# A new order table for the attention stages ahead of and inside a fused attention and MLP kernel

## The chip, the cores and the metric

The kernel runs on one core of a Trainium2 chip. The metric is the device time of one execution in microseconds (us), as a median of several runs.

## The reference

```python
def _attn_ref(q, k, v, p):                       # batch 8, heads 8, seq 576, head_dim 64, 32 packs
    p_packed = sm_attn(p, k, v)                  # 32 packed queries attend to all keys
    return sm_attn(q, p_packed, p_packed)        # all queries attend to the 32 packed rows

def _moe_ref(x, w_gate, w_val, w_out, rms_g):    # 4608 tokens, 512 -> 1536 -> 512
    xn = x / sqrt(mean(x * x) + 1e-6) * rms_g
    g = xn @ w_gate
    return (g * sigmoid(g) * (xn @ w_val)) @ w_out

def _moe2_ref(x, w_in, w_out):                   # 512 -> 2048 -> 512
    h = x @ w_in
    return maximum(0.01 * h, h) @ w_out
```

`reference()` runs the three one after the other. `sm_attn` is the scaled softmax attention; q, k and p are drawn eight times wider than v. The weights come in double precision.

## The kernel before

**Three stretches.** First come the loads, the attention of the first batches and the conversion of the first weights (here called the front). Then a main loop of 96 steps (L1207) forms the first MLP: four pairs of batches, six groups of 256 hidden columns each, two batches and two halves of a sequence. Last comes the second MLP as a matrix product with fewer multiplications, from tiles that the main loop prepared. Every product is made of three: a value is split into a rounded high part and a low part (`mm3`, `split`).

**Units.** The attention of a batch is cut into two units of four heads, so there are 16 units. `soft1` (L324) is a unit's first attention, nine stages: keys, packs, scores, exps, sums, turn, packed, packed_turn, factors. `soft2` (L468) is the second: queries, scores, maxima, shift, exps, sums, norm, turn, two squares, and for a batch's second unit means and two finals. Stages issue loads too: keys loads the next unit's k and p, queries the next q, packed the next v. From batch 1's end on, shift, norm and final run on GpSimd.

**What goes beside it.** `split_w` and `split_wo` take one tile of weights each: `convert` (L683) turns doubles into floats, one ScalarE instruction (L693) and four on VectorE (L696, L702, L713, L719); the load of a later tile follows. `fold` (L872) multiplies weights by the packed rows (pwps) and splits the result (pw), ScalarE first, VectorE last. It uses the same PSUM banks as the output products y (`y_out`, L936). `split_at` splits the attention weights that the products g and v (`gv`, L913) read. `keep_warm(n)` (L960) issues n dummy products, two matmul instructions each.

**The order.** Each stage has a step number. `ONE` and `TWO` hold those of `soft1` and `soft2`, unit by unit; SPLITW, SPLITO, FOLD0, FOLD, SPLITA and WARM those of the rest. Units 8 to 15 follow a formula:

```python
S1 = (0, -2, 2, 6, 10, 11, 13, 15, 17)
S2 = (4, 5, 6, 7, 8, 8, 10, 12, 16, 17, 22, 25, 23)
L0, LP = 78, 23
ONE += tuple(tuple(L0 + LP * i + at for at in S1) for i in range(8))
TWO += tuple(tuple(L0 + LP * (i + 1) + at for at in S2[: 10 + 3 * (i % 2)]) for i in range(8))
```

`fill_slots` (L644) enters the stages in a table, and `run_slots(end)` (L652) traces all below `end` in order of step; within a step the units come first, then dummies, split_at, weights, folds. Steps below zero are traced in one go before the main loop. In the loop `slot()` (L1013) is called four times in each of the 96 main-loop steps, so main-loop step n covers steps 4n to 4n + 3. Folds of the later pairs, the conversion of the second MLP's weights and later split_at are called from the loop itself, outside the tables.

The order of tracing is a priority. A planner at compile time orders each engine's queue with estimated times and lets ready work of later steps go first. Two calls bind it: `tc.keep_in_program_order` pins an instruction behind the one that its engine was handed last (the dummies, and before the loop the first instruction of each conversion), and `tc.issue_after` puts what follows behind a given instruction. At run time each engine works through its queue in order and waits on semaphores. All loads and stores that matter here are issued from SP's queue.

Of the kernel before, what the change touches and what calls it, by code (L numbers as in the profile page):

```python
# [15 lines left out]
DRAM = bass.MemoryType.DRAM  # L16


S1 = (0, -2, 2, 6, 10, 11, 13, 15, 17)
S2 = (4, 5, 6, 7, 8, 8, 10, 12, 16, 17, 22, 25, 23)  # L20

ONE = (
# [8 lines left out]
)  # L31
TWO = (
# [8 lines left out]
)  # L41
L0, LP = 78, 23
ONE += tuple(tuple(L0 + LP * i + at for at in S1) for i in range(8))
TWO += tuple(tuple(L0 + LP * (i + 1) + at for at in S2[: 10 + 3 * (i % 2)]) for i in range(8))
SPLITW = (-68, -58, -57, -57, -8, -6, -1, -1, 9, 10, 13, 13, 21, 29, 29, 29, 37, 37, 45, 42, 50, 53, 59, 61,)
SPLITO = (-56, -63, 3, 8, 26, 29, 33, 39, 48, 55, 67, 71,)
FOLD0 = (-36, -31, 4, 0,)
FOLD = (4, 5, 23, 31, 36, 44, 60, 55, 63, 79,)
SPLITA = (-5, -18,)
WBUFS = 8  # L50
HEAD = 2
OWN = 1
# [8 lines left out]
CUT = 3  # L61
CONV0, CONV = 25, 1.6
EVERY = (1, 1)
WARM = ([-90, 5], [-58, 5], [-49, 10], [-22, 1],)


@with_exitstack
def pack_attention_moe_kernel(
# [592 lines left out]
    def split_at(b, cs=(0, 1)):  # L661
        if b not in ath:
            ath[b] = (
                mlpa.tile([P, 2, S], F32R, tag="ath", bufs=2, name=f"ath{b}"),
                mlpa.tile([P, 2, S], F32R, tag="atl", bufs=2, name=f"atl{b}"),
            )
        h, l = ath[b]
        f = atf[b]
        assert {("at", b, 0), ("at", b, 1)} <= made
        for c in cs:  # L670
            cs = slice(c * CH, c * CH + CH)
            act_copy(h[:, :, cs], f[:, :, cs])
            sub(side[0], l[:, :, cs], f[:, :, cs], h[:, :, cs])
# [107 lines left out]
    def split_w(i):  # L781
        if i < NW:
            until(lambda: ("r", i) in wq)
            t = mlpa.tile([P, 512], F32, tag="w", bufs=WBUFS, name=f"w{i}")
            convert(wq.pop(("r", i)), t, f"w{i}", True)

            def done():
                wq["s", i] = t
                flush_store()
                stores.append((w_dram[i], t))  # L790
                if i >= 2:
                    load_w(i + 2)

            after(done)
        elif i < NPAIR * NW:
            t = mlpa.tile([P, 512], F32, tag="w", bufs=WBUFS, name=f"w{i}")
            nc.sync.dma_start(out=t, in_=w_dram[i % NW])
            wq["s", i] = t
# [14 lines left out]
    def split_wo(i):  # L813
        if i < NF1:
            until(lambda: ("r", i) in wo)
            t = mlpb.tile([P, 2, 512], F32R, tag="wo", bufs=4, name=f"wo{i}")
            convert(wo.pop(("r", i)), t, f"wo{i}")

            def done():
                wo["s", i] = t  # L820
                flush_store()
                stores.append((wo_dram[i], t))
                if i >= 1:
                    load_wo(i + 1)

            after(done)
        elif i < NPAIR * NF1:
            t = mlpb.tile([P, 2, 512], F32R, tag="wo", bufs=4, name=f"wo{i}")
            ins = nc.sync.dma_start(out=t.bitcast(F32), in_=wo_dram[i % NF1])
            tc.keep_in_program_order(ins)  # L830
            wo["s", i] = t
# [40 lines left out]
    def fold(n, u, bbs=(0, 1)):  # L872
        if n >= NPAIR * NFG:
            return
        ks = [n * KT + 2 * u + x for x in range(2)]
        until(lambda: all(("s", k_) in wq for k_ in ks))
        w = [wq["s", k_] for k_ in ks]
        outs = []
        for bb in bbs:
            if (n, bb) not in pw:  # L880
                pw[n, bb] = mlpa.tile(
                    [P, 2, 2, 2 * G * P], F32R, tag=f"pw{bb}", bufs=2, name=f"pw{n}{bb}"
                )
            outs.append(bank(f"pwps{n}{u}{bb}")[:, 0, :])
            assert ("lpw", 2 * (n // NFG) + bb, u) in made
        def part(h, bb, ps):
            r = (h ^ bb) % 2
            rs = slice(64 * r, 64 * r + 64)
            c = 32 * (h % 2)
            return nc.tensor.matmul(  # L890
                ps[32 * h : 32 * h + 32],
                lhsT=lpw[2 * (n // NFG) + bb][rs, 2 * u + h // 2, c : c + 32],
                rhs=w[h // 2][rs],
                start=True,
                stop=True,
            )

        todo = [(h, bb, ps) for h in range(4) for bb, ps in reversed(list(zip(bbs, outs)))]
        with claim(outs[:-1]):
            first = part(*todo[0])  # L900
        with tc.issue_after(first.ins):
            for x in todo[1:]:
                part(*x)
        for bb, ps in zip(bbs, outs):
            hi, lo = pw[n, bb][:, u, 0, :], pw[n, bb][:, u, 1, :]
            act_copy(hi, ps)
            sub(nc.vector, lo, ps, hi)
# [52 lines left out]
    def keep_warm(count):  # L960

        ps = psA.tile([P, 512], F32, tag="y", bufs=4, name="warm")
        for _ in range(count):
            ins = nc.tensor.matmul(
                ps[:, :256],
                lhsT=ident,
                rhs=mask.rearrange("p h d -> p (h d)"),
                start=True,
                stop=True,
            )  # L970
            tc.keep_in_program_order(ins)

    for k_, count in WARM:
        slots.setdefault(k_, []).append(lambda count=count: keep_warm(count))
# [8 lines left out]
    halves = [(lambda c=c: split_at(0, (c,))) for c in range(2)]  # L983
    table = list(zip(SPLITA, halves))
    table += [(k_, lambda i=i: split_w(i)) for i, k_ in enumerate(SPLITW)]
    table += [(k_, lambda i=i: split_wo(i)) for i, k_ in enumerate(SPLITO)]
    table += [(k_, lambda i=i: fold(0, i % 2, (i // 2,))) for i, k_ in enumerate(FOLD0)]
    table += [(k_, lambda i=i: fold(1 + i // 2, i % 2)) for i, k_ in enumerate(FOLD)]
    for k_, f_ in table:
# [486 lines left out]
```

## Time and profile before

| | us |
|---|---|
| median of 3 runs (1636.6, 1639.88, 1641.48) | 1639.88 |
| the profiled execution | 1636.23 |
| its span, first to last instruction | 1634.5 |
| TensorE (PE) busy | 1547.3 |
| VectorE (DVE) busy | 1117.9 |
| ScalarE (ACT) busy | 764.7 |
| GpSimd (POOL) busy | 598.5 |

The profile is of one execution. Times below are from the start of the span. In a timeline each row has start, duration, engine, line, operation, tiles (out<-in), shapes, count, and in brackets the idle time of the engine just before and what ended it. PE are the matmuls and PEld their weight loads; SPq is the queue that issues loads. TensorE's clock as granted is given as a share of 2.4 GHz, so 0.50 is 1.2 GHz.

### The profile page before, as it was taken

To read this page: it belongs to the slowest core of one execution; us is meant where nothing else is said; L and a number is where in the kernel's file an instruction comes from. 1 tells how busy PE (TensorE), PEld (TensorE's weight loads), DVE (VectorE), ACT (ScalarE), POOL (GpSimd) and SP (SyncE) were. 2 spreads that over 40 slices of the span, in tenths; PEclk is the share of its full clock that TensorE was granted. 3 is DMA by queue.
4 is the path that set the end of the run, shared out by engine and by line. 5 is a ranking of instruction groups with operands and counts; after the bars stand their busy time and mean duration, and the time that the engine had idled before them with its cause. 6 is when DMAs were issued, how large, how long until landed. Compare 5 with 4: busy or idle time off the path is not lost.

```text
span 1634.5 us, 29463 instructions
## 1 busy us (share of the span) xinstructions
PE 1547.3 (95%) x10760; PEld 1363.4 (83%) x10760; DVE 1117.9 (68%) x2026; ACT 764.7 (47%) x1390; POOL 598.5 (37%) x415
## 2 busy tenths in 40 slices
PE   6789889999999899999999999999999999999997
PEld 4458778878888788888999988888889998999997
DVE  7787888566767756677768549646854964784475
ACT  3365544464445554555434246346524633553452
POOL 1124334443434524355224463075017306502610
PEclk8799999999999999999999999999999999999999
DMA  8664554375556834468775666787787778778776
GB/s 264 208 185 154 187 168 132 116 231 177 174 171 220 267 108 149 162 219 312 257 262 210 225 203 201 210 287 201 204 266 241 218 228 276 212 213 255 215 212 176
DMA packets 219519, 342.22 MB, mean 209 GB/s; under 512 B 21232, under 2 KB 120560, under 8 KB 219376
## 3 DMA queue, kind: packets, MB, share of 16 engines
q1 hardware_dynamic: 217488, 339.42, 66.0%
q8 instruction: 86, 1.41, 0.4%
q10 hardware_dynamic: 1888, 0.92, 0.2%
q14 instruction: 57, 0.47, 0.1%
HBM read 266.86 MB, written 73.40 MB: 208 GB/s over the span
## 4 chain that ended last, share of the span: by engine, by line
PE 66%; DVE 14%; DMA 9%; ACT 4%; issue 3%; POOL 2%; SPq 1%; ACTq 0%; DVEq 0%; POOLq 0%
PE o L142 22%; PE h L142 20%; PE y L142 11%; PE g L142 5%; PE v L142 4%; DMA sl<-c_dram 2%; DVE y_acc L952 2%; DMA wo<-in_moe_w_out_dram 2%; DMA w<-in_moe_w_in_dram 1%; PE pwps L890 1%; DMA w<-in_moe_w_out_dram 1%; PE xp L566 1%; DMA pc<-s_dram 1%; DVE pw L167 1%; DVE cvw L713 1%
## 5 line engine op out<-in xcount | busy, mean ns | idle before, releaser
L142 PE MATMUL o<-gh,pc 128*128 128x448 f32 (+1 forms) x1120 | 324.6, 371 | 0.0
L142 PE MATMUL y<-hh,wo 128*128 128x288 f32 x1536 | 274.0, 301 | 20.4 <-DVE pw L167 13.6
L142 PE MATMUL h<-yh,pc 128*128 128x448 f32 (+1 forms) x1120 | 280.7, 372 | 4.5 <-DMA pc<-s_dram 2.6
L142 PEld LDWEIGHTS y<-hh,wo 128*128 128x128 f32 x1536 | 223.7, 189 | 50.3 <-DVE pw L167 15.1
L167 POOL TENSOR_TENSOR hl<-sg,hh 128x576 fp32r<-128x576 f32 x96 | 146.9, 1530 | 293.1 <-ACT hh L159 284.9
L142 PEld LDWEIGHTS h<-yh,pc 128*128 128x128 f32 x1120 | 209.7, 188 | 31.3 <-ACT b5h L159 2.9
L142 PEld LDWEIGHTS o<-gh,pc 128*128 128x128 f32 x1120 | 210.2, 188 | 25.0
L159 ACT ACTIVATE gh<-g 128x448 fp32r<-128x448 f32 (+1 forms) x280 | 160.8, 587 | 131.4 <-PE o L142 68.9
L167 DVE TENSOR_TENSOR gl<-g,gh 128x448 fp32r<-128x448 f32 (+1 forms) x280 | 180.2, 661 | 50.0 <-ACT gh L159 42.9
L142 PE MATMUL o<-gl,pc 128*128 128x448 f32 (+1 forms) x560 | 207.0, 371 | 0.0
L1300 POOL TENSOR_TENSOR b6h<-b6h,b5h 128x448 f32<-128x448 f32 (+1 forms) x40 | 59.0, 1475 | 348.7 <-ACT gh L159 262.9
L952 DVE TENSOR_TENSOR y_acc<-y_acc,y 128x288 f32<-128x288 f32 x320 | 139.1, 446 | 55.0 <-PE y L142 54.1
L142 PE MATMUL y<-hl,wo 128*128 128x288 f32 x768 | 164.4, 296 | 1.2 <-POOL hl L167 1.2
L142 PE MATMUL h<-yl,pc 128*128 128x448 f32 (+1 forms) x560 | 162.7, 371 | 0.0
L142 PE MATMUL g<-ath,pw 128*128 128x288 f32 x768 | 152.3, 307 | 8.4 <-ACT sg L1240 6.1
L142 PE MATMUL v<-ath,pw 128*128 128x288 f32 x768 | 145.4, 302 | 1.4 <-DVE sg L929 1.4
L142 PEld LDWEIGHTS g<-ath,pw 128*128 128x128 f32 x768 | 115.9, 189 | 31.0 <-issue 12.2
L142 PEld LDWEIGHTS y<-hl,wo 128*128 128x128 f32 x768 | 123.8, 189 | 2.3 <-POOL hl L167 2.3
L1294 POOL TENSOR_TENSOR g<-g,g 128x448 f32<-128x448 f32 (+1 forms) x80 | 116.1, 1451 | 25.0 <-ACT gh L159 13.2
L142 PEld LDWEIGHTS v<-ath,pw 128*128 128x128 f32 x768 | 115.8, 189 | 4.7 <-DVE sg L929 2.5
L142 PEld LDWEIGHTS h<-yl,pc 128*128 128x128 f32 x560 | 105.1, 188 | 12.3
L142 PEld LDWEIGHTS o<-gl,pc 128*128 128x128 f32 x560 | 105.1, 188 | 12.3
(162 smaller groups left out, 2452.6 us busy)
## 6 DMA issues: line engine op xcount, KB each, us to landing
pc<-s_dram SPq DMA_DIRECT2D x320, 256.0 KB, 3.0
pc<-w_dram SPq DMA_DIRECT2D x240, 256.0 KB, 3.0
w<-w_dram SPq DMA_DIRECT2D x72, 256.0 KB, 4.1
wo<-wo_dram SPq DMA_DIRECT2D x36, 512.0 KB, 5.1
w_dram<-w2s SPq DMA_DIRECT2D x32, 512.0 KB, 4.9
s_dram<-ss SPq DMA_DIRECT2D x32, 512.0 KB, 6.0
v<-in_v_dram SPq DMA_DIRECT2D x16, 576.0 KB, 4.9
y_dram<-y_acc SPq DMA_DIRECT2D x32, 288.0 KB, 2.6
```

Source lines behind the costliest of these rows:

```text
L142: mm = nc.tensor.matmul(ps, lhsT=lh if a == "h" else ll, rhs=rh if b == "h" else rl, start=start and i == 0, stop=stop and i == n - 1,)
L159: nc.scalar.activation(out=o, in_=i, func=AF.Copy, scale=scale)
L167: eng.tensor_tensor(out=o, in0=a, in1=hi.bitcast(F32), op=ALU.subtract)
L566: nc.tensor.matmul(xp[:, k_, :CH], lhsT=Pm[:, 2 * x : 2 * x + 2, :].rearrange("p h d -> p (h d)"), rhs=st["AT"][:, c * CS : (c + 1) * CS, ...
L713: nc.vector.scalar_tensor_tensor(out=cu, in0=hiw, scalar=0xC0000000, in1=cu, op0=ALU.bitwise_and, op1=ALU.bitwise_or)
L890: return nc.tensor.matmul(ps[32 * h : 32 * h + 32], lhsT=lpw[2 * (n // NFG) + bb][rs, 2 * u + h // 2, c : c + 32], rhs=w[h // 2][rs], star ...
L952: pace[:] = [nc.vector.tensor_tensor(out=ya, in0=ya, in1=pv, op=ALU.add).ins]
L1294: eng.tensor_tensor(out=o, in0=a, in1=b, op=ALU.subtract)
L1300: return eng.tensor_tensor(out=o, in0=a, in1=b, op=ALU.add)
```

## The change

S1, S2, L0 and LP go. ONE and TWO list all 16 units, and many numbers change; so do those of the conversions, folds, split_at and dummies. No function changes.

```diff
-    (-80, -82, -71, -66, -62, -61, -59, -57, -55,),
-    (-61, -63, -59, -55, -51, -50, -48, -46, -44,),
+    (-77, -79, -69, -69, -63, -62, -60, -58, -56,),
+    (-61, -68, -59, -55, -54, -51, -48, -47, -45,),
...
+    (78, 76, 80, 82, 88, 91, 93, 95, 97,),
+    (101, 99, 103, 107, 111, 112, 114, 116, 118,),
+    (124, 122, 126, 130, 134, 135, 137, 139, 141,),
+    (147, 145, 149, 153, 157, 158, 160, 162, 164,),
+    (170, 168, 172, 180, 180, 181, 183, 190, 192,),
+    (193, 191, 195, 199, 203, 204, 206, 208, 210,),
+    (208, 214, 218, 222, 226, 226, 228, 232, 232,),
+    (239, 224, 241, 245, 249, 250, 252, 254, 256,),
 )
 TWO = (
-    (-47, -45, -43, -43, -42, -42, -40, -40, -36, -34,),
-    (-47, -43, -43, -40, -39, -38, -37, -34, -30, -28, -25, -20, -22,),
+    (-49, -47, -45, -44, -43, -42, -40, -40, -36, -34,),
+    (-47, -43, -43, -40, -39, -39, -38, -35, -31, -29, -26, -21, -23,),
...
+    (104, 105, 106, 107, 108, 108, 110, 112, 117, 118,),
+    (123, 129, 130, 131, 132, 132, 134, 136, 140, 141, 146, 149, 147,),
+    (147, 147, 148, 149, 150, 155, 157, 159, 163, 177,),
+    (174, 175, 176, 177, 178, 178, 181, 183, 187, 188, 192, 195, 193,),
+    (194, 195, 201, 202, 203, 203, 205, 207, 211, 212,),
+    (219, 220, 221, 222, 223, 223, 225, 227, 231, 232, 237, 240, 238,),
+    (256, 257, 258, 259, 260, 260, 262, 264, 268, 269,),
+    (260, 265, 266, 267, 268, 268, 270, 272, 276, 277, 282, 285, 283,),
 )
-L0, LP = 78, 23
...
-SPLITW = (-68, -58, -57, -57, -8, -6, -1, -1, 9, 10, 13, 13, 21, 29, 29, 29, 37, 37, 45, 42, 50, 53, 59, 61,)
-SPLITO = (-56, -63, 3, 8, 26, 29, 33, 39, 48, 55, 67, 71,)
-FOLD0 = (-36, -31, 4, 0,)
-FOLD = (4, 5, 23, 31, 36, 44, 60, 55, 63, 79,)
-SPLITA = (-5, -18,)
+SPLITW = (-68, -58, -59, -57, -12, -6, -1, -1, 4, 6, 12, 13, 21, 29, 29, 29, 37, 38, 44, 42, 48, 50, 55, 56,)
+SPLITO = (-56, -65, 1, 7, 26, 29, 33, 41, 49, 53, 67, 71,)
+FOLD0 = (-38, -36, 3, -1,)
+FOLD = (4, 5, 23, 31, 35, 44, 57, 55, 63, 79,)
+SPLITA = (-18, -20,)
...
-WARM = ([-90, 5], [-58, 5], [-49, 10], [-22, 1],)
+WARM = ([-85, 5], [-53, 2], [-41, 10], [-22, 1],)
```

By the formula unit 12 had queries, scores, maxima, shift and exps of its second attention at 197, 198, 199, 200 and 201, and unit 14 at 243 to 247, with its two squares at 255 and 256; unit 14's first attention had keys at 216, and unit 15's packs stood at 237.

## Rows read from the trace of the kernel before

**Rows 1.** The page: busy time, share, count of TensorE
```profile
PE 1547.3 (95%) x10760; PEld 1363.4 (83%) x10760; DVE 1117.9 (68%) x2026; ACT 764.7 (47%) x1390; POOL 598.5 (37%) x415
```
**Rows 2.** Stretches: length, busy us (count) PE PEld DVE ACT POOL, clock, DMA, GB/s
```profile
0.00:81.00 81.00, 55.37 (x367) 38.44 (x368) 59.45 (x119) 29.27 (x54) 12.67 (x18) 0.79 0.76 236
81.00:327.00 246.00, 223.47 (x2070) 189.81 (x2071) 189.80 (x378) 127.61 (x223) 93.44 (x62) 1.00 0.49 157
327.00:905.00 578.00, 551.70 (x4903) 495.15 (x4888) 411.61 (x790) 285.20 (x515) 232.76 (x158) 0.99 0.61 206
```
**Rows 3.** Timeline of VectorE at the start
```profile
9.70 0.46 DVE L368 TENSOR_REDUCE mx<-s 128x1 f32<-128x288 f32 x1 [0.45 <-ACT e L159]
...
12.83 0.43 DVE L696 TENSOR_SCALAR w<-w 128x512 f32<-128x512 f32 x1 [2.67 <-ACT w L693]
13.17 0.21 DVE L370 TENSOR_SCALAR nb<-mx 128x1 f32<-128x1 f32 x1
...
17.91 0.43 DVE L354 STREAM_TRANSPOSE pT<-pm 128x256 f32<-128x256 f32 x1
```
**Rows 4.** Timeline: the first dummies, the third block and unit 1's packed rows
```profile
2.10 4.18 PE L964 MATMUL warm<-mask,ident 128*128 128x256 f32 x10 [2.10 <-DVE mask L181]
...
28.18 4.48 PE L964 MATMUL warm<-mask,ident 128*128 128x256 f32 x20
...
28.59 0.84 ACT L159 ACTIVATE a1T<-ta 96x384 f32<-96x384 f32 x2
...
32.59 0.88 PE L411 MATMUL pp<-v,a1T 96*32 96x64 f32 x48
...
38.73 0.47 DVE L419 SCALAR_TENSOR_TENSOR Pm<-pp,rin,mask 128x256 f32<-128x256 f32 x1
```
**Rows 5.** Stretches of 4 us at the front
```profile
28.00:32.00 4.00, 4.00 (x22) 3.56 (x21) 4.00 (x9) 1.43 (x3) 0.00 (x0) 1.00 1.07 338
...
44.00:48.00 4.00, 2.37 (x6) 1.24 (x5) 3.77 (x5) 0.00 (x0) 0.92 (x1) 0.50 0.90 226
```
**Rows 6.** Timeline from 41 us to the first products
```profile
41.48 4.21 PE L239 MATMUL s<-qT,PT 128*128 128x288 f32 x8 [1.54 <-DVE PT L443]
...
43.31 1.28 SPq L808 DMA_DIRECT2D wo<-in_moe_w_out_dram  x2
...
47.32 2.26 PE L566 MATMUL xp<-AT,Pm 128*128 128x288 f32 x4 [1.63 <-DVE AT L540]
...
51.47 0.66 ACT L693 ACTIVATE cvwo<-wo 128x512 f32<-128x512 f32 x1 [7.89 <-DMA wo<-in_moe_w_out_dram]
...
56.84 3.90 PE L239 MATMUL s<-kT,pT 128*128 128x288 f32 x8 [2.20 <-ACT sq L573]
...
62.51 2.10 PE L239 MATMUL s<-kT,pT 128*128 128x288 f32 x8
...
81.10 0.91 PE L142 MATMUL v<-ath,pw 128*128 128x288 f32 x4
```
**Rows 7.** Waits of TensorE from 327 to 905: total us, times, longest us
```profile
PE y L142 <- DVE pw L167: 10.6, 8, 2.6
```
**Rows 8.** Timeline around the wait that ends at 557.78
```profile
553.56 0.73 DVE L507 TENSOR_REDUCE mx<-sn 128x18 f32<-128x576 f32 x1
...
554.22 0.68 DVE L713 SCALAR_TENSOR_TENSOR cvw<-w,cvw 128x512 uint32<-128x512 uint32 x1
...
554.37 1.54 POOL L515 TENSOR_TENSOR sn<-sn,mx 128x576 f32<-128x576 f32 x1 [2.07 <-DVE mx L507]
...
554.82 1.64 DVE L719 SCALAR_TENSOR_TENSOR cvw<-w,cvw 128x512 uint32<-128x512 uint32 x1
...
557.04 1.28 DVE L167 TENSOR_TENSOR pw<-pwps,pw 128x512 fp32r<-128x512 f32 x2
...
557.78 0.79 PE L142 MATMUL y<-hh,wo 128*128 128x288 f32 x4 [2.46 <-DVE pw L167]
```
**Rows 9.** Timeline ahead of the wait that ends at 339.6
```profile
333.14 3.09 POOL L167 TENSOR_TENSOR atl<-atf,ath 128x576 fp32r<-128x576 f32 x2 [3.12 <-ACT ath L159]
...
333.29 3.22 DVE L702 TENSOR_SCALAR cvw<-cvw 128x512 uint32<-128x512 uint32 x2
```

More of the change, by code (lines that the diff above doesn't have):

```diff
@@ L16 @@
 DRAM = bass.MemoryType.DRAM
-S1 = (0, -2, 2, 6, 10, 11, 13, 15, 17)
-S2 = (4, 5, 6, 7, 8, 8, 10, 12, 16, 17, 22, 25, 23)
 ONE = (
[4 rows of a table removed]
[4 rows of a table added]
     (6, 4, 8, 12, 13, 17, 19, 21, 23,),
[2 rows of a table removed]
[2 rows of a table added]
     (54, 52, 56, 60, 64, 65, 67, 69, 71,),
[8 rows of a table added]
 )
 TWO = (
[4 rows of a table removed]
[4 rows of a table added]
     (25, 31, 32, 33, 34, 34, 36, 36, 42, 43,),
[3 rows of a table removed]
-)
-L0, LP = 78, 23
-ONE += tuple(tuple(L0 + LP * i + at for at in S1) for i in range(8))
-TWO += tuple(tuple(L0 + LP * (i + 1) + at for at in S2[: 10 + 3 * (i % 2)]) for i in range(8))
-SPLITW = (-68, -58, -57, -57, -8, -6, -1, -1, 9, 10, 13, 13, 21, 29, 29, 29, 37, 37, 45, 42, 50, 53, 59, 61,)
-SPLITO = (-56, -63, 3, 8, 26, 29, 33, 39, 48, 55, 67, 71,)
-FOLD0 = (-36, -31, 4, 0,)
-FOLD = (4, 5, 23, 31, 36, 44, 60, 55, 63, 79,)
-SPLITA = (-5, -18,)
[11 rows of a table added]
+)
+SPLITW = (-68, -58, -59, -57, -12, -6, -1, -1, 4, 6, 12, 13, 21, 29, 29, 29, 37, 38, 44, 42, 48, 50, 55, 56,)
[3 more added lines that the diff above has]
+SPLITA = (-18, -20,)
 WBUFS = 8
```

18 rows, old and new, of tables (ONE, TWO) are left out of this document.

## Prediction

> **What bounds the kernel now.** I read the engines' shares first, then the stretches, then what the engines waited for inside each stretch. TensorE is busy for 1547.3 us of a span of 1634.5 us, so 87 us of it are idle [rows 1]. By stretches [rows 2] the idle time is 25.6 us of the first 81 us (81.00 - 55.37, at a mean granted clock of 0.79), 22.5 us from 81 to 327 (246.00 - 223.47) and 26.3 us from 327 to 905 (578.00 - 551.70), both at a clock of 0.99 to 1.00. What is left of the 87, some 13 us, lies behind 905, in the second pair of matrix products; no step of the tables reaches it. The change issues the same instructions except for six dummy matmuls, so it can only move idle time, the time that matmuls take at half clock in the first 81 us, and a little queueing on VectorE. The upper bound is therefore about 74 us and what the clock costs at the start.
>
> The steps are not issue times. They set the order in which the planner is handed the work, and it then orders each engine's queue by its own estimate, pulling ready work forward. So I trust only moves that change what an instruction can be queued behind: a pinned one (the first ScalarE step of a conversion before the main loop, and each dummy matmul, stays behind whatever its engine was handed last), and moves of over ten steps.
>
> **The first 81 us, pinned pieces.** (1) The first weight conversion, w0, was handed over between unit 0's scores and its exponential, and is now behind the exponential. In the trace VectorE's first piece of w0 waits for ScalarE's (2.67 us idle, to 12.83) and sits ahead of unit 0's small "nb" instruction (13.17), though the maxima that nb reads were done at 9.70 + 0.46 = 10.16 [rows 3]. The exponential and the transposes behind it wait for nb: 13.17 - 10.16 = 3.0 us. With w0 pinned behind the exponential, nb can't be queued behind w0 any more: that removal is certain. How much reaches the end of the stretch is not. Unit 1's scores need its own packed keys, which VectorE transposes only at 17.91 [rows 3], so what is late next is unit 1, not unit 0. Bounds 0 and 3.0; I take 1.0, a third, since the row nearest to the end of the chain is unit 1's.
>
> (2) The block of 20 dummy matmuls (WARM's third entry) goes from ahead of unit 1's "packed" to behind unit 0's second sums, that is behind unit 1's second scores on TensorE. In the trace it runs from 28.18 for 4.48 us, while unit 1's transposed exponentials are ready at 28.59 + 0.84 = 29.43; "packed" starts at 32.59, 3.1 us late [rows 4]. But its result is scaled on VectorE only at 38.73 [rows 4], in a queue that is full: from 28 to 32 VectorE is busy 4.00 of 4.00 us [rows 5]. So bounds 0 and 3.1; the full queue is the nearest row and I take 1.0.
>
> (3) The block's new place. At its old one it keeps the clock at 1.00 from 28 to 32, but from 44 to 48 the clock is at 0.50 of full speed, 1.2 GHz, with TensorE busy 2.37 of 4 us [rows 5]. At the new place it follows unit 1's second scores (from 41.48 for 4.21 us, so to 45.7) and fills the idle time ahead of unit 0's squares at 47.32 [rows 6]. What comes after would run at full speed. On the path there is one piece: the scores of unit 2, eight matmuls, took 3.90 us from 56.84; the same eight matmuls of unit 3 took 2.10 us at 62.51, at full clock [rows 6]. That is 3.90 - 2.10 = 1.8 us gained. The other half-clock pieces are hidden: ScalarE and VectorE both stand until 51.4 because the wo load, issued at 43.31, lands then, and ScalarE sat idle 7.89 us before it [rows 6]. The bound below nothing is the first rival that ends slower.
>
> (4) The second dummy block shrinks from ten matmuls to four and moves; it is worth at most 1.5 us of TensorE ahead of unit 0's second scores, whose result VectorE takes up far later in the full queue. Nothing; bounds 0 and 1.5. The other moves there (split_at half 0 from -5 to -18, folds by one to five steps, w4 from -8 to -12, "means" by one) come behind the same instructions as before: w5, w6 and w7 stay pinned behind the same exponentials. Nothing, bounds -1 and +1 together.
>
> Sum of the front: 1.0 + 1.0 + 1.8 = 3.8 us. It carries over to everything behind, since the first products (81.10) wait for this chain [rows 6].
>
> **The main loop.** From 327 to 905 the largest wait of TensorE is that of a y product for VectorE's last read of a fold's PSUM bank: 10.6 us in 8 places, longest 2.6 [rows 7]. The folds themselves keep their places there; what stands ahead of them on VectorE moves. The clearest place is at 557.78, where the y product waited 2.46 us for the fold's subtraction at 557.04; ahead of it VectorE ran unit 12's maxima (553.56, 0.73 us) among pieces of two weight conversions, one of which took 1.64 us instead of the 0.68 us of its neighbour while GpSimd ran unit 12's shift [rows 8]. Unit 12's second queries and scores are now three steps earlier, its maxima to turn two steps later, which takes both out of this queue: 0.73 + (1.64 - 0.68) = 1.7 us. Bounds 0 and 2.46. The longest wait of this kind, 2.6 us, ends at 339.6 and has another cause: two conversion pieces took 3.22 us there while GpSimd ran two split_at subtractions for 3.09 us [rows 9], and split_at of this batch is not in the tables. Nothing. For the moves of one to five steps of units 5 to 13 I see no row that says which way they go: 0, with half of the 10.6 us, 5.3, as a bound on both sides. Units 14 and 15 are a rival.
>
> **Sum.** 3.8 + 1.7 = 5.5 us off the profiled execution of 1636.23 us gives 1630.7 us. That execution lies 3.65 us under the median of the three timed runs, 1639.88, and near their lowest, 1636.6; I place the median of the changed kernel half of that above the sum, 1.8 us: **1632.5 us**, 0.45% under 1639.88. About 0.3%, 4.9 us, is what a measurement can tell from no change.
>
> **The rivals.** Larger gain: (1) reaches the chain with half of its 3.0, (2) with all of its 3.1, (3) with 1.8, and half of the 10.6 us goes: 1.5 + 3.1 + 1.8 + 5.3 = 11.7 us, 1636.23 - 11.7 + 1.8 = 1626 us. For it speaks that 8 waits of one kind are left and that half of the units are laid out one by one for the first time; against it the full VectorE queue. Its best end is everything: 3.0 + 3.1 + 1.8 + 10.6 = 18.5, so 1619.5 us.
>
> Nothing: the planner's order comes out nearly the same, the wo load still lands at 51.4 and frees both engines then, and the waits of the loop only change place: 1638 us, between the profiled execution and the median. The trace speaks for it in that a conversion of the output weights already runs at 51.47 [rows 6], before the first products, though all but two of them are handed over at step 3 and later.
>
> Slower, by the dummy block: it starts at 45.7 with the clock at half. The first ten dummies of the kernel took 4.18 us [rows 4], so twenty can take 8.4 us and end at 54.1, 6.8 us behind the moment when unit 0's squares now start. If the clock rises only late and ScalarE's squares then become the last thing, all 6.8 us stay: 1636.23 + 6.8 + 1.8 = 1645 us. It decides from the point where the block ends after the 51.4 us at which the wo load frees ScalarE.
>
> Slower, by the crowd at the end: unit 14's second half goes from steps 243-256 to 256-269, onto unit 15's at 260-285, with four folds among them (main-loop steps 64, 65, 68, 69). If three of these waits grow to the longest, 3 x 2.6 = 7.8: 1636.23 + 7.8 + 1.8 = 1646 us. Two rows show VectorE held up while GpSimd works [rows 8, 9], and each unit's shift and norm run on GpSimd. The Trainium skill (SBUF - State Buffer, "Who interferes with whom") says that VectorE and GpSimd share one port pair as an exclusive lock, so that one blocks fully; by that rule each such meeting costs up to a whole GpSimd instruction, and the trace agrees (1.64 us beside a GpSimd instruction against 0.68 without). Against it: as much such work stood among folds before, at other steps.
>
> **How the numbers follow.** Forecast 0.40, larger gain 0.22, nothing 0.18, dummy block 0.12, crowd 0.08. Faster by over 0.3% (under 1635): 0.32 of the forecast's and all of the larger gain's, 0.54. Within 0.3%: 0.06 + 0.15 + 0.03 + 0.03 = 0.27. Slower (over 1644.8): 0.02 + 0.03 + 0.09 + 0.05 = 0.19. The range goes from under the larger gain's best end to above both slower cases, 1617 to 1648, and leaves about 0.08 below and 0.10 above. The forecast's own range, with its bounds of 5.3 on both sides, is 1627 to 1638.
>
> **What would show it.** Right: in the changed profile nb stands right behind the maxima (at about 10.4), ahead of every piece of w0; unit 1's "packed" is no longer behind twenty dummies; the clock from 48 to 60 is at 1.00 and unit 2's scores take 2.1 us; the first products start some 4 us before 81.1; the wait of y for a fold's subtraction from 327 to 905 is 8 us or less. Wrong: the first products start at 81 or later, or the loop takes back what the front gains, read as the time from the first Silu of the main loop to the last. The prediction fails as a whole if the wo load at the front lands later than 51.4, since SP's one queue carries all loads in the order of the steps, and a step that moved takes its load along.

## The result and the profile after

The changed kernel takes 1618.3 us as the median of its runs (1615.79 to 1625.12), the kernel before 1638.24 us beside it: a ratio of 0.9884, with a 95% interval from 0.9847 to 0.9922. That is 19.0 us by the ratio (19.9 by the medians), where 5.5 were forecast. The profiled execution took 1615.79 us; its span is 20.5 us shorter than that of the kernel before. It is the fastest of only four runs, which matters below: five of the kernels tried there have medians from 1622.9 to 1625.4 us, inside the spread of these four runs, so a difference of that size from the changed kernel is not clear of noise. In the new code every line behind the tables stands 11 lower (L142 is now L153, L167 is L178).

The page's line of busy time, beside [rows 1]:

```profile
PE 1538.3 (95%) x10754; PEld 1360.2 (84%) x10754; DVE 1114.7 (69%) x2026; ACT 764.4 (47%) x1390; POOL 598.1 (37%) x415
```

TensorE issues six instructions fewer, the dummies, and is busy 9 us less; the other engines do what they did. The same three stretches as in [rows 2] (length, busy us and count of PE, PEld, DVE, ACT, POOL, clock, DMA share, GB/s):

```profile
0.00:81.00 81.00, 55.26 (x388) 40.10 (x392) 60.88 (x123) 29.76 (x57) 14.17 (x19) 0.81 0.80 250
81.00:327.00 246.00, 226.94 (x2139) 193.82 (x2131) 195.28 (x385) 131.16 (x229) 98.75 (x66) 0.99 0.51 161
327.00:905.00 578.00, 559.66 (x4929) 505.96 (x4922) 414.88 (x799) 286.12 (x515) 230.97 (x156) 1.00 0.63 212
```

Each fixed stretch now holds more matmuls (388 for 367, then 2139 for 2070), so the profiled execution gets ahead in the front and again in the loop; the third (4929 for 4903) no longer compares equal work, since the loop already ends at 884. To compare equal work I cut both kernels at the first and the last sigmoid of the main loop (the instruction that applies Silu, at L1240, now L1251). First the loop of the kernel before, then that of the changed kernel:

```profile
88.20:905.70 817.50, 768.89 (x6921) 680.54 (x6922) 596.77 (x1162) 409.66 (x733) 325.29 (x219) 1.00 0.58 191
```
```profile
83.80:884.10 800.30, 763.70 (x6921) 679.49 (x6922) 597.68 (x1163) 410.03 (x733) 325.58 (x219) 1.00 0.59 196
```

So in these two executions the front gives 88.2 - 83.8 = 4.4 us and the loop 17.2; behind the loop 1.1 us are lost (728.8 to 729.9). The loop has the same 6921 matmuls, yet only 12.0 of its 17.2 us show as less idle time (817.5 - 768.9 = 48.6, to 36.6); 5.2 show as less busy time of the same instructions, with 6.8 us at half clock in both. The likely reason: ends of matmuls are modelled, and a single product shows 0.29 us where four in a row show 0.69, so each adds 0.13 and a tail of 0.16 behind the last is counted as busy. A wait as short as that tail does not show as idle time.

Cut further at the sigmoids of every twelfth step (worked out from the windows of both profiles; matmuls in brackets, since a part that has fewer of them did less):

| main-loop steps | before, us | after, us |
|---|---|---|
| 0 to 24 | 230.7 (1955) | 227.4 (1961) |
| 24 to 36 | 105.6 (945) | 103.2 (939) |
| 36 to 48 | 103.3 (928) | 101.9 (926) |
| 48 to 60 | 113.9 (977) | 106.7 (970) |
| 60 to 72 | 99.1 (852) | 92.6 (830) |
| 72 to 95 | 164.9 (1277) | 168.5 (1307) |

At the loop's mean of 0.12 us a matmul, the last two together gain 4 us (some work moved from the one into the other), steps 48 to 60 gain 6, and the three above them 7 in all. The gain is spread, with one place that stands out: steps 48 to 60, where the fold of [rows 8] is.

### The profile page after: what moved, and what is told of

It reads as the page before. It is cut to its first block, busy times and chain, and to the rows that moved or that the text cites. A ratio compares the mean times of both kernels' runs of the same rounds, so it can differ in the third digit from the quotient of the medians.

```text
span 1614.0 us, 29460 instructions
## 1 busy us (share of the span) xinstructions
PE 1538.3 (95%) x10754; PEld 1360.2 (84%) x10754; DVE 1114.7 (69%) x2026; ACT 764.4 (47%) x1390; POOL 598.1 (37%) x415
## 4 chain that ended last, share of the span: by engine, by line
PE 68%; DVE 14%; DMA 8%; ACT 4%; issue 3%; POOL 2%; SPq 1%; ACTq 0%; DVEq 0%; POOLq 0%
PE o L153 22%; PE h L153 20%; PE y L153 10%; PE g L153 5%; PE v L153 4%; DVE y_acc L963 2%; DMA w<-in_moe_w_in_dram 2%; DMA sl<-c_dram 1%; DMA pc<-s_dram 1%; PE xp L577 1%; PE pwps L901 1%; DMA w<-in_moe_w_out_dram 1%; DVE pw L178 1%; PE s L250 1%; DVE sg L940 1%
## 5 line engine op out<-in xcount | busy, mean ns | idle before, releaser
L153 PE MATMUL o<-gh,pc 128*128 128x448 f32 (+1 forms) x1120 | 324.6, 371 | 0.0
L153 PE MATMUL y<-hh,wo 128*128 128x288 f32 x1536 | 274.1, 301 | 17.0 <-DVE pw L178 7.3
L153 PE MATMUL h<-yh,pc 128*128 128x448 f32 (+1 forms) x1120 | 281.0, 372 | 4.9 <-DMA pc<-s_dram 2.0
L153 PEld LDWEIGHTS y<-hh,wo 128*128 128x128 f32 x1536 | 223.6, 189 | 44.8 <-DVE pw L178 10.1
L178 POOL TENSOR_TENSOR hl<-sg,hh 128x576 fp32r<-128x576 f32 x96 | 147.3, 1534 | 291.8 <-ACT hh L170 254.4
L153 PEld LDWEIGHTS h<-yh,pc 128*128 128x128 f32 x1120 | 209.4, 188 | 32.6 <-ACT b5h L170 4.5
L153 PEld LDWEIGHTS o<-gh,pc 128*128 128x128 f32 x1120 | 210.2, 188 | 24.8
L178 DVE TENSOR_TENSOR gl<-g,gh 128x448 fp32r<-128x448 f32 (+1 forms) x280 | 177.9, 652 | 50.7 <-ACT gh L170 44.1
L153 PE MATMUL o<-gl,pc 128*128 128x448 f32 (+1 forms) x560 | 207.0, 371 | 0.0
L153 PE MATMUL y<-hl,wo 128*128 128x288 f32 x768 | 164.0, 296 | 1.0 <-POOL hl L178 1.0
L153 PE MATMUL h<-yl,pc 128*128 128x448 f32 (+1 forms) x560 | 162.7, 371 | 0.0
L153 PE MATMUL g<-ath,pw 128*128 128x288 f32 x768 | 151.2, 307 | 4.5 <-ACT sg L1251 2.8
L153 PE MATMUL v<-ath,pw 128*128 128x288 f32 x768 | 147.3, 303 | 2.5 <-DVE sg L940 2.5
L153 PEld LDWEIGHTS g<-ath,pw 128*128 128x128 f32 x768 | 116.4, 189 | 25.3 <-issue 10.5
L153 PEld LDWEIGHTS y<-hl,wo 128*128 128x128 f32 x768 | 123.5, 189 | 2.3 <-POOL hl L178 2.3
L153 PEld LDWEIGHTS v<-ath,pw 128*128 128x128 f32 x768 | 115.8, 188 | 7.6 <-DVE sg L940 3.7
L153 PEld LDWEIGHTS o<-gl,pc 128*128 128x128 f32 x560 | 105.1, 188 | 12.5
L153 PEld LDWEIGHTS h<-yl,pc 128*128 128x128 f32 x560 | 105.1, 188 | 12.4
```

The lines of the kernel that those rows point to most:

```text
L153: mm = nc.tensor.matmul(ps, lhsT=lh if a == "h" else ll, rhs=rh if b == "h" else rl, start=start and i == 0, stop=stop and i == n - 1,)
L178: eng.tensor_tensor(out=o, in0=a, in1=hi.bitcast(F32), op=ALU.subtract)
```

## The experiments

All experiments change numbers of the tables and nothing else. A time in brackets behind a ratio is that kernel's median beside the median of the kernel before in the same comparison; a gain in us is worked out from the ratio, with 1638 us for the kernel before. "Old steps" of units 8 to 15 are those of the formula, written out in the diffs.

### Which half of the tables carries the gain

**front_only**: the kernel before with the new numbers for all that has a step below zero, the dummies, FOLD0 and SPLITA.

```diff
-    (-80, -82, -71, -66, -62, -61, -59, -57, -55,),
+    (-77, -79, -69, -69, -63, -62, -60, -58, -56,),
...
-WARM = ([-90, 5], [-58, 5], [-49, 10], [-22, 1],)
+WARM = ([-85, 5], [-53, 2], [-41, 10], [-22, 1],)
```

> The kernel before with the new numbers of everything handed over before the main loop (all steps below zero, the dummies, FOLD0 and SPLITA), the loop's steps as before. Theory (the front gives its own 4 us and the loop the other 16): about 1634 us, 0.3% under before, with the first Silu of the main loop at about 84 us instead of 88 and nothing more gained behind it. Rival (the loop only gains because it starts from another state): 1620 us, most of the whole gain. Rival (the front's 4 us are eaten by a later wait): 1638 us.

Ratio 0.9985, 0.9963 to 1.0007 (1636.44 beside 1638.7): 2.5 us off, and no gain at all is inside the interval. **loop_only** is the other half: the changed kernel with the front of the kernel before.

```diff
-    (-77, -79, -69, -69, -63, -62, -60, -58, -56,),
+    (-80, -82, -71, -66, -62, -61, -59, -57, -55,),
...
-WARM = ([-85, 5], [-53, 2], [-41, 10], [-22, 1],)
+WARM = ([-90, 5], [-58, 5], [-49, 10], [-22, 1],)
```

> The changed kernel with the front of before. Theory (parts add): about 1622 us, some 4 us over the changed kernel, the first Silu at 88. Rival (front and loop need each other): 1630 us or more.

Ratio 0.9905, 0.9871 to 0.994 (1623.26): 15.6 us. **late_units** is the kernel before with nothing new but units 8 to 15.

```diff
-    (78, 76, 80, 84, 88, 89, 91, 93, 95,),
+    (78, 76, 80, 82, 88, 91, 93, 95, 97,),
...
-    (216, 214, 218, 222, 226, 227, 229, 231, 233,),
-    (239, 237, 241, 245, 249, 250, 252, 254, 256,),
+    (208, 214, 218, 222, 226, 226, 228, 232, 232,),
+    (239, 224, 241, 245, 249, 250, 252, 254, 256,),
...
```

> The kernel before with the new steps of units 8 to 15 alone. Theory (the loop's gain lies with the units that followed the formula): 1638 - 12 = 1626 us, with the wait of y for a fold's last subtraction halved behind 318 us. Rival (the gain lies in the first pair's units and conversions, steps 0 to 100): 1636 us or more.

Ratio 0.9909, 0.9884 to 0.9933 (1622.94): 14.9 us. So the units that the formula laid out alike carry some four fifths of the gain; the new steps of units 5 to 7, of the first folds and of the conversions in the loop add nothing to it that can be measured (14.9 with units 8 to 15 alone, 15.6 with them too).

The profiles say the same more sharply once the first 24 main-loop steps are left out. From the sigmoid of step 24 to the last, the kernels with the old units 8 to 15 take 586.4 to 588.9 us (586.8 before, 586.4 front_only, 588.5 w0_only, 588.9 warm_only), and those with all the new ones 572.9 to 575.7 (572.9 in the changed kernel, 574.3 in no_warm and w5_early, 574.5 in loop_only, 575.7 in late_units): 11 to 16 us, whatever the front. Up to step 24 the profiles scatter, from 227.4 to 237.3 us, with the changed kernel's the shortest of all.

### Unit 12's second attention

**two12_only** moves it alone in the kernel before; **no_two12** takes it alone back in the changed kernel (the same diff, the other way round).

```diff
-    (197, 198, 199, 200, 201, 201, 203, 205, 209, 210,),
+    (194, 195, 201, 202, 203, 203, 205, 207, 211, 212,),
```

> The kernel before with the new steps of unit 12's second attention alone. Theory (unit 12's maxima and shift leave the queue ahead of the fold at 557, which removes the wait of 2.46 us and the stretch at half clock that follows it): 4 us off, about 1634.5 us, all of it between 528 and 586, and no stretch at 0.50 of the clock there. Rival (it takes the other units of the stretch too): 1638 us, the wait stands.

> The changed kernel with unit 12's second attention back on the formula's steps. Theory: 4 us lost, 1622 us, with a wait of over 2 us for a fold near 545 and half clock behind it. Rival (the other moves clear the queue on their own): 1618 us, as the changed kernel.

Alone: 0.9979, 0.9953 to 1.0004 (1633.45 beside 1638.91), 3.4 us. Taken back: 0.9934, 0.991 to 0.9958 (1626.06), against 0.9884 with it, so 0.5% or 8 us, though the two intervals just overlap. From step 24 to the last sigmoid the profiles give the same two sizes: 3.4 us (583.4 for 586.8) and 8.0 (580.9 for 572.9). The timeline of no_two12 shows what [rows 8] showed (start, duration, engine, line, tiles, idle before):

```profile
551.80 0.74 DVE L518 TENSOR_REDUCE mx<-sn 128x18 f32<-128x576 f32 x1
...
552.62 1.53 POOL L526 TENSOR_TENSOR sn<-sn,mx 128x576 f32<-128x576 f32 x1 [4.61 <-DVE mx L518]
...
553.13 1.57 DVE L730 SCALAR_TENSOR_TENSOR cvw<-w,cvw 128x512 uint32<-128x512 uint32 x1
...
554.90 0.75 DVE L536 TENSOR_REDUCE sm<-sn 128x18 f32<-128x576 f32 x1 [0.20 <-ACT sn L532]
...
555.91 0.69 DVE L178 TENSOR_TENSOR pw<-pwps,pw 128x512 fp32r<-128x512 f32 x1
...
556.65 1.27 PE L153 MATMUL y<-hh,wo 128*128 128x288 f32 x4 [3.59 <-DVE pw L178]
...
558.20 1.16 PE L153 MATMUL y<-hh,wo 128*128 128x288 f32 x4
```

Unit 12's maxima stand ahead of the fold's subtraction once more, a conversion piece takes 1.57 us beside GpSimd's shift, and y waits 3.59 us. Unit 12's sums (554.90) stand ahead of it too; in the kernel before they came behind it, at 558.24. And there is a part that the prediction had not counted, in the window right behind the wait:

```profile
556.80:560.20 3.40, 3.40 (x15) 3.40 (x16) 1.43 (x3) 3.00 (x6) 1.38 (x2) 0.51 0.85 297
```

The granted clock is at half until 560.2: four products take 1.16 us there, not the 0.69 us that they take at full clock. That is 3.4 x 0.5 = 1.7 us more. In the kernel before the wait of 2.46 us has the same sequel (half clock from 558.7 to 562.1).

All the profiles together tell this place best. The wait of y for this one fold's subtraction, read from each kernel's timeline of TensorE (waits under 0.9 us not told apart):

| unit 12's second attention | kernels and their wait at this fold, us |
|---|---|
| old steps | before 2.46, front_only 2.46, warm_only 2.45, only_1415 2.62, only_8to11 2.96, no_two12 3.59, w0_only 3.81 |
| new steps | two12_only 1.37; under 0.9 in late_units, loop_only, no_1415, no_warm, w5_early and the changed kernel |

No other part of the change separates the two rows. In the changed kernel a conversion piece still takes 1.57 us beside GpSimd, ahead of the same fold:

```profile
541.55 1.41 POOL L542 TENSOR_TENSOR A<-sn,sm 128x576 f32<-128x576 f32 x1 [1.75 <-DMA wo<-wo_dram]
...
541.94 1.57 DVE L724 SCALAR_TENSOR_TENSOR cvw<-w,cvw 128x512 uint32<-128x512 uint32 x1
...
545.30 1.27 DVE L178 TENSOR_TENSOR pw<-pwps,pw 128x512 fp32r<-128x512 f32 x2
```

What changed is the queue: in the 7 us ahead of the subtraction there are no unit's maxima and no transposed scores, it comes 6.1 us behind its fold's matmuls (539.16 to 545.30) instead of 7.2 (548.74 to 555.91 in no_two12), and no y has to wait for it.

### Units 8 to 11 and units 14 and 15

**only_8to11**: the kernel before with the new steps of units 8 to 11 (unit 10's queries to exps four or five steps earlier and its second square 13 later, unit 9's queries five earlier, the rest by one or two).

```diff
-    (128, 129, 130, 131, 132, 132, 134, 136, 140, 141, 146, 149, 147,),
-    (151, 152, 153, 154, 155, 155, 157, 159, 163, 164,),
+    (123, 129, 130, 131, 132, 132, 134, 136, 140, 141, 146, 149, 147,),
+    (147, 147, 148, 149, 150, 155, 157, 159, 163, 177,),
...
```

> The kernel before with the new steps of units 8 to 11 alone. If the gain of units 8 to 15 (16 us) is a sum, these give what units 12 and 14 to 15 leave: about 5 us, 1633 us, most of it between main-loop steps 24 and 48. Rival (units 12 to 15 hold all of it): 1638 us.

Ratio 1.001, 0.9993 to 1.0026 (1639.33 beside 1637.92): nothing. Its profile gains 2.1 us in steps 24 to 36 (103.5 for 105.6), and gives back 4.7 in steps 48 to 60 (118.6 for 113.9), where unit 12 stands at its old place:

```profile
556.54 0.96 PE L153 MATMUL y<-hh,wo 128*128 128x288 f32 x4 [2.96 <-DVE pw L178]
...
562.75 0.80 PE L153 MATMUL g<-ath,pw 128*128 128x288 f32 x4 [2.03 <-ACT sg L1251]
```

Both waits are followed by a stretch at half clock (557.0 to 560.4 and 563.8 to 567.3).

**only_1415** is the kernel before with the new steps of units 14 and 15, **no_1415** the changed kernel without them.

```diff
-    (243, 244, 245, 246, 247, 247, 249, 251, 255, 256,),
-    (266, 267, 268, 269, 270, 270, 272, 274, 278, 279, 284, 287, 285,),
+    (256, 257, 258, 259, 260, 260, 262, 264, 268, 269,),
+    (260, 265, 266, 267, 268, 268, 270, 272, 276, 277, 282, 285, 283,),
```

> The kernel before with the new steps of units 14 and 15 alone. Theory (unit 14's delay relieves the folds of main-loop steps 58 to 66): 3 to 5 us off, 1634 us, gained between main-loop steps 60 and 84. Rival (the crowd costs): 1642 us. Rival (nothing on its own): 1638 us.

> The changed kernel with units 14 and 15 back on the formula. Theory (unit 14's second half, 13 steps later, relieves the folds around main-loop steps 58 to 66): 1618 + 6 = 1624 us. Rival (the crowd of units 14 and 15 costs time, as the prediction's last rival has it): 1612 us. No effect: 1618 us.

Alone: 0.9989, 0.9972 to 1.0007 (1637.1 beside 1637.92). Taken back: 0.9911, 0.9879 to 0.9943 (1623.04), some 4 us slower than the changed kernel. The intervals of the changed kernel and of no_1415 overlap, so a gain is not shown, but the crowd that the prediction feared at the end costs nothing. In the profiles, too, y's waits in the later steps (from 605 to 780 us in no_1415, from 601 to 777 in the changed kernel; us in total, times, longest) are longer in no_1415, shown first:

```profile
PE y L153 <- DVE pw L178: 2.4, 2, 1.4
...
PE y L153 <- POOL hl L178: 1.2, 1, 1.2
```
```profile
PE y L153 <- DVE pw L178: 1.1, 3, 0.4
PE y L153 <- POOL hl L178: 0.7, 1, 0.7
```

The parts are not additive, by their medians: unit 12's second attention 3.4 us, units 8 to 11 -1.6 and units 14 and 15 1.8 make 3.6 us, and all late units together 14.9. What is missing from the sum is unit 12's first attention and unit 13, moved by up to five steps, which were not tried by themselves, and what the parts do to each other: unit 12's move is worth 3.4 us in the old table and 8 in the new (the intervals are several us wide). And with unit 12's second attention at its old place the rest of the change still gives 10.8 us (no_two12). How the remainder is shared between the two is open.

### The pieces of the front

**w0_only**: the kernel before with only the first conversion behind unit 0's exponential.

```diff
-SPLITW = (-68, -58, -57, -57, -8, -6, -1, -1, 9, 10, 13, 13, 21, 29, 29, 29, 37, 37, 45, 42, 50, 53, 59, 61,)
+SPLITW = (-65, -58, -57, -57, -8, -6, -1, -1, 9, 10, 13, 13, 21, 29, 29, 29, 37, 37, 45, 42, 50, 53, 59, 61,)
```

> The kernel before with the first weight conversion handed over at -65 instead of -68, behind unit 0's exponential. Theory (prediction's part 1): nb at 10.4 instead of 13.17, the first transposes of unit 0 at about 11.6 instead of 14.40, and 1 us off at the first Silu (87 instead of 88). Rival (the whole 3 us reach the main loop): first Silu at 85. Other rival (loads and the full VectorE queue hide it): first Silu at 88.

Ratio 0.9993, 0.9972 to 1.0013 (1636.8 beside 1638.91). nb runs at 10.73 instead of 13.17 and the first sigmoid comes at 86.5 instead of 88.2, but in the time this can't be told from nothing.

**warm_only**: the kernel before with the new dummies alone. **no_warm** is the changed kernel with the old ones (the same diff backwards).

```diff
-WARM = ([-90, 5], [-58, 5], [-49, 10], [-22, 1],)
+WARM = ([-85, 5], [-53, 2], [-41, 10], [-22, 1],)
```

> The kernel before with the new dummies alone (WARM). Theory (parts 2 to 4): unit 1's packed rows 3 us earlier on TensorE, full clock from 48 to 60, unit 2's scores in 2.1 us, and some 3 us off at the first Silu (85). Rival (the block at its new place holds up unit 0's squares): first Silu at 90 or later. Other rival (hidden): 88.

> The changed kernel with the dummies of before (WARM), all other steps as changed. The dummies alone made the kernel before 6 us slower. Theory (the new dummies pay only with the other moves of the front, which bring unit 0's chain forward in VectorE's queue): slower than the changed kernel, about 1622 us, TensorE at half clock from 37 to 54 again. Rival (the new dummies cost time in either kernel): faster, 1614 us.

warm_only is slower, 1.0037, 1.0018 to 1.0056 (1643.89 beside 1638.91, 6 us): the prediction's rival with the dummy block, as a kernel of its own. no_warm: 0.9917, 0.9893 to 0.9942 (1625.42), some 5 us slower than the changed kernel, with overlapping intervals (four runs each). So the new dummies cost time in the old table and cost none in the new; that they gain there is not shown. TensorE's timeline of warm_only, against [rows 4, 6]:

```profile
30.91 1.51 PE L422 MATMUL pp<-v,a1T 96*32 96x64 f32 x48 [3.05 <-DMA v<-in_v_dram]
...
47.08 4.67 PE L975 MATMUL warm<-mask,ident 128*128 128x256 f32 x20
...
53.85 1.85 PE L577 MATMUL xp<-AT,Pm 128*128 128x288 f32 x4 [2.10 <-DVE AT L551]
...
62.58 2.21 PE L250 MATMUL s<-kT,pT 128*128 128x288 f32 x8 [2.78 <-ACT sq L584]
```

Unit 0's squares start at 53.85, 6.5 us later than before (47.32), where the rival said 6.8. But the block, done at 51.75, is not what they wait for last; that is AT, and ScalarE's and VectorE's timelines show why:

```profile
50.75 0.68 ACT L704 ACTIVATE cvwo<-wo 128x512 f32<-128x512 f32 x1 [6.40 <-DMA wo<-in_moe_w_out_dram]
...
51.46 0.43 DVE L707 TENSOR_SCALAR cvwo<-cvwo 128x512 f32<-128x512 f32 x1 [6.60 <-ACT cvwo L704]
...
52.97 0.73 DVE L551 STREAM_TRANSPOSE AT<-A 128x576 f32<-128x576 f32 x1
```

With the block ahead of the squares the planner seems to have had no more reason to hurry AT, and queued it behind a piece of wo whose load lands at 50.7; in the kernel before, AT stood ahead of that piece (46.44 in its timeline). That the planner's estimate did this is argued; that AT stands behind the piece is shown.

**w5_early** tries to improve the changed kernel: one of the conversions ahead of the main loop, w5, goes six steps earlier.

```diff
-SPLITW = (-68, -58, -59, -57, -12, -6, -1, -1, 4, 6, 12, 13, 21, 29, 29, 29, 37, 38, 44, 42, 48, 50, 55, 56,)
+SPLITW = (-68, -58, -59, -57, -12, -12, -1, -1, 4, 6, 12, 13, 21, 29, 29, 29, 37, 38, 44, 42, 48, 50, 55, 56,)
```

> The changed kernel with the sixth weight conversion (w5) handed over at -12 behind w4, instead of -6 behind unit 2's second exponential. In the changed kernel w5's first piece runs at 81.30, its last frees the tile for the load of w7 at 90.28, w7 is converted from 94.23, and main-loop step 2 waits for it (Silu 1 at 88.3, Silu 2 at 107.0). Theory (that pin sets the hole at main-loop step 2): w7 loads at about 80, Silu 2 comes at 101, and the kernel takes 1613 us. Rival (VectorE is full there, so w5's four pieces push unit 2's chain and the first products back by as much): Silu 0 at 86 or later and 1618 us. Other rival (w8 and w9 wait in turn, the hole moves to the next main-loop step): 1617 us.

Ratio 0.9904, 0.9879 to 0.9929 (1623.7): no better than the changed kernel. The forecast of 1613 us failed: the first sigmoid comes at 88.3 instead of 83.8, as its rival with the full VectorE queue had it (86 or later), but other executions of the changed front come as late (below), so that rival is not shown either. No version beat the changed kernel.

## Why the prediction was right in sign and too small

The time lies in the range (1617 to 1648), at its lower end, and below the best end of the rival with the larger gain (1619.5). The sum itself, 5.5 us, was less than a third of the gain; that the range held owes to how wide the rivals made it, and so in part to luck. The signs named for "right" all hold in the profile: nb, the dummies, the clock, unit 2's scores, the first products and 6.3 us of waits for a fold. Step by step:

**(1) w0 behind the exponentials: right.** VectorE's timeline of the changed kernel, against [rows 3]:

```profile
10.04 0.46 DVE L379 TENSOR_REDUCE mx<-s 128x1 f32<-128x288 f32 x1 [0.45 <-ACT e L170]
10.54 0.21 DVE L381 TENSOR_SCALAR nb<-mx 128x1 f32<-128x1 f32 x1
...
16.48 0.38 DVE L707 TENSOR_SCALAR w<-w 128x512 f32<-128x512 f32 x1
```

nb follows the maxima at once and w0 is 6 us behind. The term was 1.0 us; w0_only measured 1.1 with an interval that holds zero, so its size stays open.

**(2) Dummies away from unit 1's packed rows: right, and for a reason more than the one given.** In the changed kernel:

```profile
29.95 1.51 PE L422 MATMUL pp<-v,a1T 96*32 96x64 f32 x48 [2.36 <-DMA v<-in_v_dram]
...
37.74 0.47 DVE L430 SCALAR_TENSOR_TENSOR Pm<-pp,rin,mask 128x256 f32<-128x256 f32 x1
```

"packed" starts 2.6 us earlier than in [rows 4], not 3.1, since now the load of v is late. And as forecast VectorE's full queue takes most of it: Pm comes 38.73 - 37.74 = 1.0 us earlier.

**(3) The block's new place: the price fits this profile, what it hangs on was missed.** The block, the squares and the scores of units 2 and 3 in the changed kernel, then ScalarE's first piece of wo, and the clock by stretches of 4 us:

```profile
44.48 5.24 PE L975 MATMUL warm<-mask,ident 128*128 128x256 f32 x20
...
50.65 2.21 PE L577 MATMUL xp<-AT,Pm 128*128 128x288 f32 x8
...
53.85 2.21 PE L250 MATMUL s<-kT,pT 128*128 128x288 f32 x8
...
58.11 2.10 PE L250 MATMUL s<-kT,pT 128*128 128x288 f32 x8
...
47.86 0.68 ACT L704 ACTIVATE cvwo<-wo 128x512 f32<-128x512 f32 x1 [4.80 <-DMA wo<-in_moe_w_out_dram]
```
```profile
44.00:48.00 4.00, 4.00 (x15) 3.35 (x14) 2.70 (x3) 0.14 (x1) 0.70 (x1) 0.75 1.05 405
48.00:52.00 4.00, 4.00 (x22) 2.41 (x22) 3.39 (x7) 2.39 (x4) 0.00 (x0) 1.00 1.03 392
52.00:56.00 4.00, 4.00 (x20) 1.94 (x18) 3.83 (x6) 1.97 (x5) 1.27 (x1) 1.00 0.84 271
56.00:60.00 4.00, 3.99 (x17) 3.15 (x17) 3.01 (x7) 3.16 (x6) 0.00 (x0) 1.00 0.15 51
```

The clock is full from 48 on, and unit 2's scores take 2.21 us instead of 3.90 [rows 6], 1.7 us for the 1.8 of the sum. But the squares, too, are 3.3 us later than before, and the scores behind them still 3.0 us earlier: the wait of 2.20 us for ScalarE's squaring [rows 6] is gone, since the wo load lands at 47.86 and not at 51.47 and ScalarE is free early, though the load is issued at the same time (43.16, before 43.31). In warm_only, where it lands at 50.7, the block costs. I named the landing as the point that decides, but as a cause of failure only. From issue to ScalarE's start the load takes 4.6 to 5.5 us in the six kernels with the new dummies and 7.6 to 8.7 in the eight with the old; why is open.

Nor does the price hold in every execution. no_two12 and w5_early have the dummies at the new place, and unit 2's scores take 3.64 and 3.89 us; late_units, two12_only and no_warm have them at the old place, and the scores take 2.21. So the half clock that the sum priced comes and goes with either place, and how much of the 1.8 us belongs to the move is not shown.

**The front in all: not settled.** Forecast 3.8 us; this profile says 4.4 (the first products at 76.58 instead of 81.10, the first sigmoid at 83.76 instead of 88.20), the time of front_only 2.5 with an interval from below zero to 6.1. But the four kernels that share the new front reach the first sigmoid at 83.8 (the changed kernel), 86.0 (no_1415), 87.1 (front_only) and 89.2 us (no_two12), and the six that share the old one between 86.9 and 89.1. The means, 86.5 and 88.0, are 1.5 us apart; the profile of the changed kernel is the earliest of its kind, and that it met the forecast so closely is luck.

```profile
76.58 0.98 PE L153 MATMUL v<-ath,pw 128*128 128x288 f32 x4
...
83.76 0.65 ACT L1251 ACTIVATE sg<-g 128x576 f32<-128x576 f32 x1
```

**The loop: the step that failed.** The term of 1.7 us for unit 12 named the right place and the right mechanism, and was mis-sized. I subtracted two instructions of VectorE from a queue; the runs show 3.4 us alone and 8 in the new table. Missing were the rest of the wait (2.46 us, not 1.7), the half clock behind it (1.7 us, which stood in the trace of before from 558.7 to 562.1, unread: the prediction looked for half clock in the first 81 us alone), and that the planner can put unit 12's sums ahead of the subtraction as well. That is so in no_two12 and in w0_only, where the order around this fold differs from that of before in nothing else and y waits 3.81 us instead of 2.46.

The term of 0 for the moves of one to five steps of units 5 to 13 failed as well: the late units together give 14.9 us, of which unit 12's second attention and units 14 and 15 explain 5.2 by themselves. Where the rest comes from stays open. The bound of 5.3 us was drawn from one kind of wait. That kind did fall as the larger gain's rival said, from 10.6 us [rows 7] to 6.3 in the same steps (311 to 884 in the changed kernel):

```profile
PE y L153 <- DVE pw L178: 6.3, 8, 2.2
```

This is 4.3 of the loop's 17.2 us. Others fell too (g's wait for ScalarE's sigmoid, from the first to the last step, from 6.1 to 2.8 us), some rose, and 5.2 us are less busy time, likely waits too short to show as idle.

**The rivals.** Larger gain: the nearest to the time, but more than half of its sum (6.4 of 11.7 us) lay in the front, and the runs have most of the gain in the loop. Nothing: false, though its argument (the front hangs on the wo load) is true of the front. Dummy block: true of the edit by itself, not in the changed kernel. Crowd of units 14 and 15: false.

By the Trainium skill (SBUF - State Buffer, "Who interferes with whom") VectorE and GpSimd share one port pair as an exclusive lock. The rows agree again: a piece took 1.57 us beside GpSimd in the changed kernel, as in no_two12, and 0.68 us at 543.43 with GpSimd idle. But in the changed kernel this meeting cost TensorE nothing that shows, since no y waited for the fold behind it.

## What to carry to other kernels

Where steps only rank work for a planner, price a move by the whole wait at the place that it empties, with the clock behind it, and not by the instructions that leave the queue; then test the moves in groups, since what each gives by itself did not add up: three groups alone gave 3.6 us, all late units together 14.9. A formula that lays out all units alike can put one of them at a bad place with respect to the folds: look for the longest waits of the loop first. Dummy matmuls placed ahead of real work have to be judged together with the queues around them: the same block cost 6 us in one table and none in the other. And read a front from several executions: one profile of it showed a gain of 4.4 us where the means over several executions were 1.5 apart.

## What the runs showed of the hardware

**A stall in the middle of a dense loop can be followed by half clock.** Behind waits of TensorE in the loop the granted clock fell to 1.2 GHz: in the kernel before at 340.2 to 343.6 and 558.7 to 562.1 (behind waits of 2.6 and 2.46 us), in no_two12 at 556.7 to 560.2 (3.59), in only_8to11 at 557.0 to 560.4 and 563.8 to 567.3 (2.96 and 2.03), in the changed kernel at 199.6 to 203.0 and 431.7 to 435.1 (1.68 and 1.71). Each cost about 1.7 us. It does not follow from the wait's length alone: in front_only a wait of 2.46 us at the same place had no such sequel (the clock stays at 1.00 from 560 to 572), nor had one of 2.06 us in no_two12 (1.00 from 521 to 525).

**The start differs between executions of one order.** no_two12, no_1415 and the changed kernel have the same order of instructions on TensorE, VectorE and ScalarE up to about main-loop step 48, yet in their profiled executions the first sigmoid comes at 89.2, 86.0 and 83.8 us and step 12 is reached at 212.6, 207.3 and 204.3. So a front must be judged by medians, and a few us in one profile of it carry no weight. Why was not settled; the load of wo, which lands at 51.81, 50.08 and 47.86 us, differs in the same order.
